# w_in rounded by GpSimd's integer add and split by ScalarE's copy and VectorE's subtraction, in place of sums on TensorE

## The chip, the core and the metric

The kernel runs on one core of one Trainium2 chip. The core's engines are TensorE (PE in the profile, its weight loads PEld), VectorE (DVE), ScalarE (ACT), GpSimd (POOL) and SyncE (SP), which here issues all DMA transfers. The metric is the device time of one execution in microseconds (us). The kernel before took 1277.62 us, the median of three runs from 1276.24 to 1278.96.

## The reference

Three blocks follow each other. The inputs have 8 batches of 8 heads with 576 rows of 64; the rows come out as 4608 tokens of 512.

```python
k_p, v_p = mean of k, v over groups of 8 rows              # 72 pooled rows
attn = softmax(q @ k_p.T / sqrt(64)) @ v_p                 # attention
x = attn as (4608, 512)
h = x @ w_in                                               # first MLP, w_in (512, 1024)
solu = h * softmax(h);  x = layernorm(solu) * g_ln @ w_out
out = ((x @ w1) * (x @ w2)) @ w3 @ w_out                   # second MLP
```

The weights of both MLPs arrive as 64-bit floats; the kernel reads them as pairs of 32-bit words and rounds them to 32-bit floats itself. Matrix products run on pairs of reduced floats (a high part and the low rest), three products for each.

## The kernel before

**Stages.** First come attention and the first MLP, interleaved by an order written out by hand; then the second MLP. The work is cut into slots. A function is put into a slot with `put`, sixteen slots make one unit of 256 tokens, and `HEAVY` names the products that TensorE does in each slot. The instructions of TensorE and the DMA issues of SyncE stand in that order. Those of VectorE, ScalarE and GpSimd are put in order by a scheduler within what the dependences allow. Each engine then works through its own row of instructions strictly in order.

**The first 50 us.** The heavy products cannot begin before two things are there: w_in, and the attention output of the first 256 tokens. The attention of these tokens has two halves of 128 tokens. For each half ScalarE takes exponentials of the scores (line 487), GpSimd multiplies them with the reciprocals of their sums (lines 507 and 514, the products called pr), TensorE transposes the products (pt, px), ScalarE copies the rounded high part (pth, line 539) and VectorE subtracts it for the low part (ptl, line 543). GpSimd also sums the tail of v (line 300) and spreads it over heads (vlh and VLL, lines 422 and 423). Then twenty products called av (line 571) follow on TensorE, and after them the first products with w_in (line 602).

**Rounding w_in.** w_in (`Win`) is cut into eight pieces of 128 by 512, numbered 0 to 7. For each piece SyncE loads 512 KB (line 157). ScalarE, for pieces 3 and 5 VectorE, takes the absolute value of the upper words; VectorE clamps it (line 206), shifts it (line 207) and merges sign and top bit into it (line 213), masks the exponent out of it (line 214) and scales the lower words with that (line 215). ScalarE copies the upper part rounded to the reduced format (`upper`, line 218). TensorE adds upper part, minus the copy, and lower part in PSUM with products against the identity and its negative (`store`, lines 223 to 225), and ScalarE copies the sum as the low rest (line 226). The slots of the loads and steps are `WIN_SLOTS`, those of `store` `WIN_STORE`.

**Rounding the other weights.** `Rounded`, which w_out, w1, w2, w3 and the last matrix use, does it otherwise: GpSimd scales the lower words to an integer (line 168), VectorE clamps, shifts and merges (lines 173, 174 and 177), and GpSimd adds the two as integers (`total`, line 183).

Of the kernel before, what the change touches and what calls it, by code (L numbers as in the profile page):

```python
# [8 lines left out]
F32 = mybir.dt.float32  # L9
F32R = mybir.dt.float32r  # L10
I32 = mybir.dt.int32
U32 = mybir.dt.uint32
AF = mybir.ActivationFunctionType
ALU = mybir.AluOpType
# [4 lines left out]
def attention_moe_kernel(  # L19
# [25 lines left out]
    nc = tc.nc  # L45

    B, H, S, D = q.shape
    P = 128
# [14 lines left out]
    F64_LO = 2.0**-15  # L63
    F64_HI = 122879.9921875

    PSUM = bass.MemoryType.PSUM
    const = ctx.enter_context(tc.tile_pool(name="const", bufs=1))
# [8 lines left out]
    def bankm(name):  # L76
        return PS.tile([P, 512], F32, tag="bm", name=name, bufs=3)
# [3 lines left out]

    ident = const.tile([P, P], F32, tag="ident", name="ident")
    make_identity(nc, ident)
    negid = const.tile([P, P], F32R, tag="negid", name="negid")
    nc.scalar.activation(negid, ident, AF.Copy, scale=-1.0)

    mask8 = const.tile([P, H], F32, tag="mask8", name="mask8")
    m16 = const.tile([P, 16], F32, tag="m16", name="m16")
# [10 lines left out]
    def split(hi, lo, src):  # L99
        nc.scalar.activation(hi, src, AF.Copy)  # L100
        nc.vector.tensor_tensor(lo, src, hi.bitcast(F32), ALU.subtract)

    def weight_pair(pool, tag, shape, name):
        return (
            pool.tile(shape, F32R, tag=tag + "h", name=name + "h"),
            pool.tile(shape, F32R, tag=tag + "l", name=name + "l"),
        )
# [6 lines left out]
    def at(t, i):  # L114

        n = t.shape[2] // 512
        return t[:, i // n, (i % n) * 512 : (i % n) * 512 + 512]
# [11 lines left out]
    def put(slot, fn, *args, first=5):  # L129
        assert now is None or slot > now  # L130
        events.setdefault(slot, []).append((first, len(events.get(slot, ())), fn, args))
# [19 lines left out]
    class Rounded:  # L151
# [13 lines left out]
        def bits(self):  # L165

            m, b, hi = self.m, self.b, self.hi = *self.scratch(), self.t[:, :, 1]
            nc.gpsimd.tensor_scalar(m, self.t[:, :, 0].bitcast(U32), 2.0**-29, 1.0, ALU.mult, ALU.mult)
            if self.abs_on_act:
                nc.scalar.activation(b.bitcast(F32), hi.bitcast(F32), AF.Abs)  # L170
            else:
                nc.vector.tensor_scalar(b, hi, 0x7FFFFFFF, None, ALU.bitwise_and)
            nc.vector.tensor_scalar(b.bitcast(F32), b.bitcast(F32), F64_LO, F64_HI, ALU.max, ALU.min)
            nc.vector.tensor_scalar(b, b, 3, 0x3FFFFFFF, ALU.logical_shift_left, ALU.bitwise_and)

        def rest(self):
            nc.vector.scalar_tensor_tensor(self.b, self.hi, -0x40000000, self.b, ALU.bitwise_and, ALU.bitwise_or)  # L177
# [8 lines left out]
    win = weight_pair(wp, "w16", [P, 4, F], "win")  # L186
    gw = [M.tile([P, FC, C], F32R, tag=t, name=t, bufs=1) for t in ("gwh", "gwl")]

    class Win(Rounded):
# [5 lines left out]
        def scratch(self):  # L195
            return [S1.tile([P, 512], I32, tag=t, name=t, bufs=4) for t in ("cvm", "cvb")]

        def bits(self):

            m, b = self.m, self.b = self.scratch()  # L200
            mf = m.bitcast(F32)
            if self.abs_on_act:
                nc.scalar.activation(mf, self.t[:, :, 1].bitcast(F32), AF.Abs)
            else:
                nc.vector.tensor_scalar(m, self.t[:, :, 1], 0x7FFFFFFF, None, ALU.bitwise_and)
            nc.vector.tensor_scalar(mf, mf, F64_LO, F64_HI, ALU.max, ALU.min)
            nc.vector.tensor_scalar(b, m, 3, 0x3FFFFFFF, ALU.logical_shift_left, ALU.bitwise_and)

        def rest(self):

            m, b, hi, lo = self.m, self.b, self.t[:, :, 1], self.t[:, :, 0]
            mf = m.bitcast(F32)
            nc.vector.scalar_tensor_tensor(b, hi, -0x40000000, b, ALU.bitwise_and, ALU.bitwise_or)
            nc.vector.tensor_scalar(m, b, -0x800000, None, ALU.bitwise_and)
            nc.vector.scalar_tensor_tensor(mf, lo.bitcast(U32), 2.0**-52, mf, ALU.mult, ALU.mult)

        def upper(self):
            nc.scalar.activation(at(win[0], self.i), self.b.bitcast(F32), AF.Copy)

        def store(self):  # L220
            hi, lo = at(win[0], self.i), at(win[1], self.i)
            s = bankm(f"w{self.i}")
            nc.tensor.matmul(s, ident, self.b.bitcast(F32), start=True, stop=False)
            nc.tensor.matmul(s, negid, hi, start=False, stop=False)
            nc.tensor.matmul(s, ident, self.m.bitcast(F32), start=False, stop=True)
            nc.scalar.activation(lo, s, AF.Copy)

    class Gw(Rounded):

# [448 lines left out]

    H0 = (-9, 2)
    T0 = (8, 13)  # L680
    WIN_STORE = (-31, -27, -25, -24, -22, -20, -18, -17)

    WIN_SLOTS = (-44, -38, -33, -31, -29, -26, -24, -21)
    GW_SLOTS = range(-8, 24, 4)
    KEPT_SLOTS = 22, 236
# [3 lines left out]

    def convert(pc, s_, load=None):  # L690
        put(s_ - 5 if load is None else load, pc.load, first=5 if load is None else 8)
        if isinstance(pc, Win):
            steps = (pc.bits, 0), (pc.rest, 1), (pc.upper, 2), (pc.store, WIN_STORE[pc.i] - s_)
        else:
            steps = (pc.bits, 0), (pc.rest, 1), (pc.total, 2), (getattr(pc, "store", None), 3)
        for fn, i in steps:
            if fn:
                put(s_ + i, fn, first=8)

# [29 lines left out]
    for i, pc in enumerate(pieces(Win, w_in) + gws):  # L729
        pc.abs_on_act = i in ABS_ON_ACT  # L730
        if i < 8:
            convert(pc, WIN_SLOTS[i], -47 + i)
        else:
            convert(pc, GW_SLOTS[i - 8])
# [6 lines left out]
    for i, pc in enumerate(bg):  # L741
        convert(pc, KEPT_SLOTS[0] + (KEPT_SLOTS[1] - KEPT_SLOTS[0]) * i // len(bg))
    units = [Unit(u) for u in range(NU)]
    for un in units:
        s_ = SLOTS * un.u
# [138 lines left out]
    for m in range(FC):  # L884
# [6 lines left out]
        if m in BLOCKS_AT:  # L891
            i = BLOCKS_AT.index(m)
# [206 lines left out]
```

## Time and profile before

| | |
|---|---|
| median of three runs | 1277.62 us (1276.24 to 1278.96) |
| the profiled execution | 1279.12 us, of which its span is 1277.3 us |
| TensorE busy | 1232.1 us (96%) |
| VectorE, ScalarE, GpSimd busy | 755.5 us (59%), 525.8 us (41%), 432.9 us (34%) |
| chain that ended last | TensorE 69%, VectorE 12%, DMA 9%, ScalarE 3%, GpSimd 2% |

The share of busy time is over the whole span. The change touches about the first 45 us, so the rows below are mostly from there: the chain of waits (followed back from the last instruction, at each step to what released it), the groups of instructions by form, and single instructions in order of time. A row in order of time gives start and duration in us; a bracket at its end gives how long the engine sat idle before it and what ended that.

### The profile page before, as it was taken

Reading aid. Unit: us, or ns where it says so; the run is one execution under the profiler, and the core shown is the slowest. Engines: PE = TensorE matmul, PEld = TensorE weight load, DVE = VectorE, ACT = ScalarE, POOL = GpSimd, SP = SyncE. Lnnn points to the kernel's source line nnn. Section 1 sums busy time; section 2 is a strip of 40 time slices with the busy share of each in tenths; the row PEclk is TensorE's granted clock in tenths of the full one; section 3 lists DMA queues with packets and bytes.
Section 4 is the critical chain, followed back from the end, with each engine's and each line's share of the span. In section 5 each row is a group of like instructions: output and inputs, shape, how many; then the busy total and the mean of one; then the engine's idle time right before and its main releaser. Section 6 shows DMA issues by size and latency. Waiting matters only on the chain.

```text
span 1277.3 us, 21834 instructions
## 1 busy us (share of the span) xinstructions
PE 1232.1 (96%) x8278; PEld 1125.1 (88%) x8278; DVE 755.5 (59%) x1497; ACT 525.8 (41%) x1480; POOL 432.9 (34%) x547
## 2 busy tenths in 40 slices
PE   7879999999999999999999999999999999999998
PEld 5668889898889888988998899999999999999997
DVE  6777576766767675545357555555454545454544
ACT  5654666665666666644344221212121212121211
POOL 3444535353535353310000142515152524242411
PEclk9989999999999999999999999999999999999999
DMA  9564546464646454214033102020101020101000
GB/s 231 123 153 116 140 130 159 117 163 116 160 133 165 131 164 107 83 42 140 26 131 117 33 1 67 1 67 1 67 1 67 2 66 1 67 1 67 5 31 34
DMA packets 85753, 109.42 MB, mean 86 GB/s; under 512 B 43664, under 2 KB 43664, under 8 KB 85648
## 3 DMA queue, kind: packets, MB, share of 16 engines
q1 hardware_dynamic: 85648, 108.03, 30.2%
q8 instruction: 65, 1.06, 0.4%
q14 instruction: 40, 0.33, 0.1%
HBM read 78.65 MB, written 29.36 MB: 85 GB/s over the span
## 4 chain that ended last, share of the span: by engine, by line
PE 69%; DVE 12%; DMA 9%; ACT 3%; issue 3%; POOL 2%; SPq 2%; POOLq 0%; DVEq 0%; ACTq 0%
PE p L959 9%; PE p L961 9%; PE p L960 9%; PE h L602 7%; PE acc L1005 5%; PE acc L1008 5%; PE acc L1007 5%; DMA f<-in_moe_w_dram 4%; PE x L660 3%; PE x L661 2%; PE x L659 2%; DMA f<-in_moe_w_out_dram 2%; DMA kv<-in_v_dram 2%; PE lt L645 2%; PE av L571 2%
## 5 line engine op out<-in xcount | busy, mean ns | idle before, releaser
L979 POOL TENSOR_TENSOR a<-a,b 128x256 f32<-128x256 f32 x72 | 52.9, 735 | 478.9 <-DVE b L978 478.9
L963 ACT ACTIVATE p<-p 128x256 f32<-128x256 f32 x72 | 27.9, 387 | 397.4 <-PE p L961 365.4
L659 PE MATMUL x<-lnh,gwh 128*128 128x256 f32 x576 | 167.2, 290 | 0.3 <-DVE lnl L649 0.3
L660 PE MATMUL x<-lnl,gwh 128*128 128x256 f32 x576 | 163.6, 284 | 2.5 <-DVE lnl L649 2.5
L661 PE MATMUL x<-lnh,gwl 128*128 128x256 f32 x576 | 163.5, 284 | 0.0
L660 PEld LDWEIGHTS x<-lnl,gwh 128*128 128x128 f32 x576 | 110.7, 192 | 3.8 <-DVE lnl L649 2.9
L1008 PE MATMUL acc<-wfl,ph 128*128 128x512 f32 x288 | 113.1, 393 | 0.0
L1007 PE MATMUL acc<-wfh,ph 128*128 128x512 f32 x288 | 112.9, 392 | 0.0
L659 PEld LDWEIGHTS x<-lnh,gwh 128*128 128x128 f32 x576 | 110.7, 192 | 1.7 <-DVE lnl L649 0.9
L661 PEld LDWEIGHTS x<-lnh,gwl 128*128 128x128 f32 x576 | 110.6, 192 | 0.0
L487 ACT ACTIVATE ea<-sc,mx 128x72 f32<-128x72 f32 x320 | 98.4, 332 | 15.3 <-DVE mx L484 15.3
L978 DVE TENSOR_TENSOR b<-b,p 128x256 f32<-128x256 f32 x72 | 30.2, 420 | 123.0 <-PE p L961 123.0
L602 PE MATMUL h<-winh,xh 128*128 128x512 f32 x288 | 98.5, 423 | 0.0
L602 PE MATMUL h<-winl,xh 128*128 128x512 f32 x288 | 90.0, 394 | 0.0
L602 PE MATMUL h<-winh,xl 128*128 128x512 f32 x288 | 89.4, 392 | 0.0
L507 POOL TENSOR_TENSOR pr<-ea,sm 128x512 f32<-128x512 f32 x40 | 42.8, 1070 | 122.7 <-DVE sm L503 71.4
L183 POOL TENSOR_TENSOR cvb<-cvb,cvm 128x512 int32<-128x512 int32 x48 | 62.7, 1306 | 59.9 <-DVE cvb L177 29.4
L959 PE MATMUL p<-th,w1h 128*128 128x256 f32 x288 | 81.6, 283 | 1.1 <-ACT p L963 1.1
L1005 PE MATMUL acc<-wfh,pl 128*128 128x512 f32 x288 | 82.4, 392 | 0.0
L960 PE MATMUL p<-th,w1h 128*128 128x256 f32 x288 | 81.5, 283 | 0.0
L961 PE MATMUL p<-th,w1l 128*128 128x256 f32 x288 | 81.5, 283 | 0.0
L649 DVE TENSOR_TENSOR lnl<-lt,lnh 128x512 fp32r<-128x512 f32 x72 | 49.1, 686 | 51.8 <-ACT lnh L648 51.4
(206 smaller groups left out, 3674.6 us busy)
## 6 DMA issues: line engine op xcount, KB each, us to landing
f<-in_moe_w_dram SPq DMA_DIRECT2D x32, 512.0 KB, 5.9
x2d<-xo SPq DMA_DIRECT2D x36, 256.0 KB, 2.0
xq<-x2d SPq DMA_DIRECT2D x36, 256.0 KB, 3.9
out_dram<-ot SPq DMA_DIRECT2D x36, 256.0 KB, 2.7
kv<-in_k_dram SPq DMA_DIRECT2D x32, 256.0 KB, 3.8
q<-in_q_dram SPq DMA_DIRECT2D x32, 256.0 KB, 7.7
kv<-in_v_dram SPq DMA_DIRECT2D x32, 256.0 KB, 3.7
f<-in_moe_w_out_dram SPq DMA_DIRECT2D x16, 512.0 KB, 5.9
```

The source lines that it names most:

```text
L183: nc.gpsimd.tensor_tensor(self.b, self.b, self.m, ALU.add)
L487: nc.scalar.activation(e[0:n, x], half[a][:, h], AF.Exp, bias=mx[0:n, x : x + 1], scale=1.0, accum_out=sm[0:n, x : x + 1],)
L602: nc.tensor.matmul(self.ph[:, a], s_[:, c], w_[:, c, a * 512 : a * 512 + 512], start=first, stop=last)
L659: nc.tensor.matmul(o, gw[0][:, f, ws], self.th[:, f], start=(f == 0), stop=False)
L660: nc.tensor.matmul(o, gw[0][:, f, ws], self.tl[:, f], start=False, stop=False)
L661: nc.tensor.matmul(o, gw[1][:, f, ws], self.th[:, f], start=False, stop=(f == FC - 1))
L959: nc.tensor.matmul(o, wh[:, c, fsl], th[:, c], start=c == 0, stop=False)
L960: nc.tensor.matmul(o, wh[:, c, fsl], tl[:, c], start=False, stop=False)
L961: nc.tensor.matmul(o, wl[:, c, fsl], th[:, c], start=False, stop=c == 1)
L1005: nc.tensor.matmul(accs[t], pl[:, ts], wh, start=False, stop=(fc == FC - 1))
L1007: nc.tensor.matmul(accs[t], ph[:, ts], wh, start=(fc == 0), stop=False)
L1008: nc.tensor.matmul(accs[t], ph[:, ts], wl, start=False, stop=False)
```

## The change

`Win` loses its own `bits`, `rest`, `upper` and most of `store`, and inherits the steps of `Rounded`: for each of the eight pieces GpSimd scales the lower words and adds them as integers (lines 168 and 183 of the kernel before). The result is split by `split` (lines 99 to 101): ScalarE copies the rounded high part, VectorE subtracts it. The table `WIN_STORE` and the constant `negid` go; the split stands three slots after the clamp, as for the other weights.

```diff
--- before.py
+++ after.py
@@ -81,8 +81,6 @@
 
     ident = const.tile([P, P], F32, tag="ident", name="ident")
     make_identity(nc, ident)
-    negid = const.tile([P, P], F32R, tag="negid", name="negid")
-    nc.scalar.activation(negid, ident, AF.Copy, scale=-1.0)
 
     mask8 = const.tile([P, H], F32, tag="mask8", name="mask8")
     m16 = const.tile([P, 16], F32, tag="m16", name="m16")
@@ -195,35 +193,8 @@
         def scratch(self):
             return [S1.tile([P, 512], I32, tag=t, name=t, bufs=4) for t in ("cvm", "cvb")]
 
-        def bits(self):
-
-            m, b = self.m, self.b = self.scratch()
-            mf = m.bitcast(F32)
-            if self.abs_on_act:
-                nc.scalar.activation(mf, self.t[:, :, 1].bitcast(F32), AF.Abs)
-            else:
-                nc.vector.tensor_scalar(m, self.t[:, :, 1], 0x7FFFFFFF, None, ALU.bitwise_and)
-            nc.vector.tensor_scalar(mf, mf, F64_LO, F64_HI, ALU.max, ALU.min)
-            nc.vector.tensor_scalar(b, m, 3, 0x3FFFFFFF, ALU.logical_shift_left, ALU.bitwise_and)
-
-        def rest(self):
-
-            m, b, hi, lo = self.m, self.b, self.t[:, :, 1], self.t[:, :, 0]
-            mf = m.bitcast(F32)
-            nc.vector.scalar_tensor_tensor(b, hi, -0x40000000, b, ALU.bitwise_and, ALU.bitwise_or)
-            nc.vector.tensor_scalar(m, b, -0x800000, None, ALU.bitwise_and)
-            nc.vector.scalar_tensor_tensor(mf, lo.bitcast(U32), 2.0**-52, mf, ALU.mult, ALU.mult)
-
-        def upper(self):
-            nc.scalar.activation(at(win[0], self.i), self.b.bitcast(F32), AF.Copy)
-
         def store(self):
-            hi, lo = at(win[0], self.i), at(win[1], self.i)
-            s = bankm(f"w{self.i}")
-            nc.tensor.matmul(s, ident, self.b.bitcast(F32), start=True, stop=False)
-            nc.tensor.matmul(s, negid, hi, start=False, stop=False)
-            nc.tensor.matmul(s, ident, self.m.bitcast(F32), start=False, stop=True)
-            nc.scalar.activation(lo, s, AF.Copy)
+            split(at(win[0], self.i), at(win[1], self.i), self.f)
 
     class Gw(Rounded):
 
@@ -678,8 +649,6 @@
 
     H0 = (-9, 2)
     T0 = (8, 13)
-    WIN_STORE = (-31, -27, -25, -24, -22, -20, -18, -17)
-
     WIN_SLOTS = (-44, -38, -33, -31, -29, -26, -24, -21)
     GW_SLOTS = range(-8, 24, 4)
     KEPT_SLOTS = 22, 236
@@ -689,11 +658,7 @@
 
     def convert(pc, s_, load=None):
         put(s_ - 5 if load is None else load, pc.load, first=5 if load is None else 8)
-        if isinstance(pc, Win):
-            steps = (pc.bits, 0), (pc.rest, 1), (pc.upper, 2), (pc.store, WIN_STORE[pc.i] - s_)
-        else:
-            steps = (pc.bits, 0), (pc.rest, 1), (pc.total, 2), (getattr(pc, "store", None), 3)
-        for fn, i in steps:
+        for fn, i in ((pc.bits, 0), (pc.rest, 1), (pc.total, 2), (getattr(pc, "store", None), 3)):
             if fn:
                 put(s_ + i, fn, first=8)
```

The order of the instructions changes with it on four engines; that of SyncE stays. Three places are shown. In them cvb and cvm are the scratch tiles of a piece, winh and winl the two parts of w_in, and pieces 5, 6 and 7 are cvb_301, cvb_329 and cvb_389 now; pieces 6 and 7 were cvb_347 and cvb_409, and the sums of 5, 6 and 7 on TensorE w_413, w_433 and w_440.

GpSimd before, from the first half's probability products to VLL:

```order
L507 TENSOR_TENSOR pr0_0_291<-ea0_0_262,sm0_0_261 128x512
L514 TENSOR_TENSOR pr0_0_291<-ea0_0_262,sm0_0_261 128x64 x2
L300 TENSOR_TENSOR vl0_181<-vl0_181 128x256
L300 TENSOR_TENSOR vl0_181<-vl0_181 128x128
L300 TENSOR_TENSOR vl0_181<-vl0_181 128x64
L422 TENSOR_TENSOR vlh0_337<-vl0_181,mask8_73 128x512
L507 TENSOR_TENSOR pr0_1_365<-ea0_1_314,sm0_1_313 128x512
L514 TENSOR_TENSOR pr0_1_365<-ea0_1_314,sm0_1_313 128x64 x2
L423 TENSOR_TENSOR VLL_113<-sl0_334,mask8_73 64x512
```

GpSimd now, from the second half's products on:

```order
L478 TENSOR_TENSOR pr0_1_348<-ea0_1_308,sm0_1_307 128x512
L271 TENSOR_TENSOR vl0_178<-vl0_178 128x256
L485 TENSOR_TENSOR pr0_1_348<-ea0_1_308,sm0_1_307 128x64 x2
L271 TENSOR_TENSOR vl0_178<-vl0_178 128x128
L271 TENSOR_TENSOR vl0_178<-vl0_178 128x64
L393 TENSOR_TENSOR vlh0_324<-vl0_178,mask8_71 128x512
L181 TENSOR_TENSOR cvb_301<-cvb_301,cvm_300 128x512
L394 TENSOR_TENSOR VLL_111<-sl0_321,mask8_71 64x512
L166 TENSOR_SCALAR cvm_328<-f64_183 128x512
L166 TENSOR_SCALAR cvm_388<-f64_185 128x512
L181 TENSOR_TENSOR cvb_329<-cvb_329,cvm_328 128x512
L181 TENSOR_TENSOR cvb_389<-cvb_389,cvm_388 128x512
```

Three integer adds and two scalings of lower words now stand in the same row as the second half's products and the v tail; pieces 6 and 7 end it.

ScalarE before, up to the last copy from the sums on TensorE:

```order
L226 ACTIVATE winl_102<-w4_387 128x512
L218 ACTIVATE winh_101<-cvb_347 128x512
L218 ACTIVATE winh_101<-cvb_409 128x512
L100 ACTIVATE VBDh_107<-vs1_0_395 64x2x64 x2
L226 ACTIVATE winl_102<-w5_413 128x512
L539 ACTIVATE pth0_351<-pt0_1_421 128x4x128
L540 ACTIVATE ptx0_353<-px0_1_426 128x128
L226 ACTIVATE winl_102<-w6_433 128x512
L226 ACTIVATE winl_102<-w7_440 128x512
```

ScalarE now, over the same part of the program:

```order
L168 ACTIVATE cvb_329<-f64_183 128x512
L98 ACTIVATE winh_99<-cvb_301 128x512
L168 ACTIVATE cvb_389<-f64_185 128x512
L98 ACTIVATE winh_99<-cvb_329 128x512
L98 ACTIVATE winh_99<-cvb_389 128x512
L98 ACTIVATE VBDh_105<-vs1_0_373 64x2x64
L510 ACTIVATE pth0_334<-pt0_1_395 128x4x128
L98 ACTIVATE VBDh_105<-vs1_0_373 64x2x64
L511 ACTIVATE ptx0_336<-px0_1_400 128x128
```

The copy pth of the second half stood between copies of pieces 5 and 6 taken from TensorE's sums; it now stands behind the rounded copies of pieces 6 and 7, which need GpSimd's last adds.

TensorE before, from the second half of the v sums to the first av product:

```order
L352 MATMUL vs_0_395<-kv_1_188,ident 128x128 x8
L223 MATMUL w_413<-cvb,ident 128x512
L224 MATMUL w_413<-winh,negid 128x512
L225 MATMUL w_413<-cvm,ident 128x512
L532 MATMUL pt_1_421<-ident,pr_1_365 128x128 x4
L535 MATMUL px_1_426<-ident,pr_1_365 128x128
L223 MATMUL w_433<-cvb,ident 128x512
L224 MATMUL w_433<-winh,negid 128x512
L225 MATMUL w_433<-cvm,ident 128x512
L223 MATMUL w_440<-cvb,ident 128x512
L224 MATMUL w_440<-winh,negid 128x512
L225 MATMUL w_440<-cvm,ident 128x512
```

TensorE now, the same part:

```order
L323 MATMUL vs_0_373<-kv_1_187,ident 128x128 x8
L503 MATMUL pt_1_395<-ident,pr_1_348 128x128 x4
L506 MATMUL px_1_400<-ident,pr_1_348 128x128
L542 MATMUL av_0_413<-pth_334,VBDh 128x256
L542 MATMUL av_0_413<-ptl_335,VBDh 128x256
```

The sums called w are gone, and av follows px at once.

## Rows read from the trace of the kernel before

**Rows 1.** us, busy by engine (PE to POOL), clock, DMA, GB/s

```profile
400.00:800.00 400.00, 391.26 (x2579) 355.58 (x2579) 229.12 (x430) 183.41 (x476) 93.44 (x118) 1.00 0.29 89
```

**Rows 2.** chain of waits, 10 to 95 us: start, duration, what

```profile
40.63 0.30 DVE VBDl L101
...
41.07 1.10 PE w L223 x2
...
44.34 0.86 PE w L225 x2
...
45.20 2.40 PE av L571 x20
...
50.02 1.37 PE h L602 x6
...
79.46 1.22 ACT ea L487 x8
...
88.38 0.69 DVE gwl L251
```

**Rows 3.** VectorE by form, 10 to 46 us: count, busy us, mean ns

```profile
L213 DVE SCALAR_TENSOR_TENSOR cvb<-f,cvb 128x512 int32<-128x512 int32 x8 | 6.3, 793 | 0.1
L215 DVE SCALAR_TENSOR_TENSOR cvm<-f,cvm 128x512 f32<-128x512 uint32 x8 | 5.5, 690 | 0.1
L206 DVE TENSOR_SCALAR cvm<-cvm 128x512 f32<-128x512 f32 x8 | 3.9, 489 | 7.5 <-ACT cvm L203 7.4
L207 DVE TENSOR_SCALAR cvb<-cvm 128x512 int32<-128x512 int32 x8 | 3.4, 422 | 0.1
L214 DVE TENSOR_SCALAR cvm<-cvb 128x512 int32<-128x512 int32 x8 | 3.4, 422 | 0.1
L484 DVE TENSOR_REDUCE mx<-sc 128x4 f32<-128x288 f32 x4 | 1.8, 453 | 0.0
```

**Rows 4.** ScalarE by form, 10 to 46 us

```profile
L218 ACT ACTIVATE winh<-cvb 128x512 fp32r<-128x512 f32 x8 | 5.1, 632 | 4.7 <-DVE cvb L213 4.7
```

**Rows 5.** GpSimd in order of time: start, us, engine, line, what

```profile
26.79 1.36 POOL L507 TENSOR_TENSOR pr<-ea,sm 128x512 f32<-128x512 f32 x1 [16.98 <-DVE sm L503]
...
34.99 1.03 POOL L423 TENSOR_TENSOR VLL<-sl,mask 64x512 fp32r<-64x512 f32 x1
...
40.63 0.65 POOL L168 TENSOR_SCALAR cvm<-f 128x512 int32<-128x512 uint32 x1 [4.60 <-DMA f<-in_moe_w_out_dram]
...
45.02 1.29 POOL L183 TENSOR_TENSOR cvb<-cvb,cvm 128x512 int32<-128x512 int32 x1 [3.75 <-DVE cvb L177]
...
53.66 1.04 POOL L507 TENSOR_TENSOR pr<-ea,sm 128x512 f32<-128x512 f32 x1 [0.43 <-DVE sm L503]
...
132.57 1.04 POOL L507 TENSOR_TENSOR pr<-ea,sm 128x512 f32<-128x512 f32 x1
133.57 0.55 POOL L514 TENSOR_TENSOR pr<-ea,sm 128x64 f32<-128x64 f32 x2
134.08 0.45 POOL L300 TENSOR_TENSOR vl<-vl 128x128 f32<-128x128 f32 x1
...
135.74 0.32 POOL L300 TENSOR_TENSOR vl<-vl 128x64 f32<-128x64 f32 x1
```

**Rows 6.** VectorE in order of time

```profile
16.39 0.18 DVE L397 COPY bdt<-pkl 64x32 f32<-64x32 f32 x1 [0.92 <-PE pkl L388]
...
53.28 0.20 DVE L503 RECIPROCAL sm<-sm 128x8 f32<-128x8 f32 x1
...
53.72 1.26 DVE L173 TENSOR_SCALAR cvb<-cvb 128x512 f32<-128x512 f32 x1 [0.23 <-ACT cvb L170]
```

**Rows 7.** TensorE in order of time, the wait before the row in brackets

```profile
80.72 0.41 PE L571 MATMUL av<-pth,VBDh 128*128 128x320 f32 x1 [2.36 <-ACT ea L487]
```

**Rows 8.** busy times, 82 to 86 us; clock third from the end

```profile
82.00:84.00 2.00, 2.00 (x11) 1.96 (x10) 1.85 (x6) 1.08 (x4) 0.34 (x1) 0.57 0.00 0
84.00:86.00 2.00, 2.00 (x12) 1.76 (x11) 2.00 (x8) 1.28 (x3) 2.00 (x3) 0.58 0.66 141
```

## The prediction

> **What bounds the kernel now.** I read the busy times by stretch first. From 400 to 800 us TensorE is busy 391 of 400 us at full clock [rows 1]: the reader is to see that, once the heavy products run, nothing but TensorE's own work counts, so a change of the start moves the end by as much as it moves the first heavy product. That one comes at 50.02 us, behind the twenty av products at 45.20 [rows 2]. The chain of waits shows what held av: VectorE's last low part of v ends at 40.93, then TensorE makes the sums of pieces 6 and 7 from 41.07 to 45.20, and av is the next in its row [rows 2]. Before that VectorE's conversion of w_in is the chain; its groups [rows 3] say what each step takes. Then I looked at what GpSimd does meanwhile, since the change gives it work: idle for 16.98 us until 26.79, busy without a gap to 36.02, and idle for 4.60 us until a load lands at 40.63 [rows 5].
>
> **What goes.** On TensorE 24 products of eight sums; the last two pieces alone are the 4.13 us between 41.07 and 45.20. On VectorE per piece a mask of 0.42 and a scaling of 0.69 [rows 3] for a subtraction from two tiles in SBUF, 0.69 like that of w_out [rows 2]: 0.42 us net, 3.4 us for eight. On ScalarE one copy of two goes. Were this all, av would come earlier, by at most 4.13 + 3.4 = 7.5 us.
>
> **What comes.** On GpSimd eight scalings of 0.65 and eight adds of 1.29 [rows 5], 15.5 us, beside the 9.23 us from 26.79 to 36.02. That fits into its idle time; the dependences are the trouble: each piece now goes VectorE merge, GpSimd add, ScalarE copy, VectorE subtraction, and each engine works strictly in its order. In the orders shown, the second half's products and the v tail share GpSimd's row with pieces 5 to 7, and ScalarE's pth copy stands behind the rounded copies of pieces 6 and 7. So av, which had to wait for VectorE and TensorE, now waits for GpSimd's very last add for w_in. I follow this path in three legs, first without any mutual disturbance. Clamp and shift are 0.42 each, a merge 0.69 (the means of lines 206 and 213 hold delayed ones), a row maximum 0.45 [rows 3], a copy on ScalarE 0.63 [rows 4], a reciprocal 0.20 [rows 6], the scaling before it as much.
>
> Leg 1, to the first half's products. VectorE's small copy for k at 16.39 [rows 6] stands ahead of the merge of piece 1, which ends at 17.3; handover 0.14 (as from 40.93 to 41.07 [rows 2]), add 1.29, copy 0.63, subtraction 0.69: 20.05. Behind it in VectorE's row up to the reciprocal stand three clamps or masks, two shifts, a maximum, a merge, the scaling and the reciprocal: 3 x 0.42 + 2 x 0.42 + 0.45 + 0.69 + 0.2 + 0.2 = 3.65, and a handover. The products start at 23.9, where they now start at 26.79 [rows 5]. So far the change gains 2.9 us.
>
> Leg 2, to the second half's products. GpSimd: products 1.04 and 0.55, scaling 0.65, add of piece 3 1.29 = 3.53. ScalarE copies it (0.63), VectorE subtracts (0.69) and only then merges piece 4 (0.69), GpSimd adds (1.29), ScalarE copies (0.63). Then VectorE has a subtraction, a mask, the scaling, a clamp and the reciprocal (0.69 + 0.42 + 0.2 + 0.42 + 0.2 = 1.93), beside which ScalarE's last three of four exponentials (three quarters of 1.22 [rows 2]) are hidden. With 0.4 for handovers that is 9.8: 33.7.
>
> Leg 3, to av, is GpSimd's row as printed: 1.04, the v tail's first sum (0.7, between the 0.45 of half its size and the 1.04 of twice), 0.55, 0.45, 0.32, vlh 1.04 (the size of pr), add of piece 5 1.29, VLL 1.03, two scalings 1.30, two adds 2.58 [rows 5] = 10.3. ScalarE then copies piece 7 (0.63), a quarter of a microsecond of v, and pth (0.6); VectorE subtracts ptl (0.69) and av's second product can run. With handovers 12.7: 46.4, so 1.2 us later than 45.20. The gain of leg 1 is used up and more.
>
> **Mutual disturbance.** The trace shows what VectorE and GpSimd do to each other. A clamp of 0.42 took 1.26 at 53.72, until just before the products that began at 53.66 ended at 54.70 [rows 5, 6]. GpSimd suffers too: the row from pr to VLL printed for before would take 6.7 us by the undisturbed durations of leg 3 (1.04 + 0.55 + 0.7 + 0.45 + 0.32 + 1.04 + 1.04 + 0.55 + 1.03) and took 9.23 [rows 5], a factor of 1.37. GpSimd's part of legs 2 and 3 is 3.53 + 1.29 + 10.3 = 15.1 us. Undisturbed it adds nothing; with that factor it adds 5.6 and av comes at 52.0. Below nothing it cannot go, as the durations are the shortest seen. VectorE's row in legs 2 and 3 is made largely of the same operations as in that stretch, but it also stands waiting for ScalarE, and then disturbs nobody. I take two thirds, 3.7 us: av at 50.1, 4.9 late.
>
> The Trainium skill, "SBUF — State Buffer", section "Who interferes with whom", says that of the two the second to issue fully blocks until the first ends. The 1.26 us row agrees. By that rule alone the whole 5.6 would stand, and av would be 6.8 late.
>
> **The clock.** With the sums gone, TensorE has little to do between the first scores and av: v sums and transpositions, with pauses. The trace shows what such a pause does: after a wait of 2.36 us [rows 7] the granted clock of 82 to 86 us is 0.57 and 0.58 [rows 8], that is (0.43 + 0.42) x 2 / 0.5 = 3.4 us at 1.2 instead of 2.4 GHz with TensorE busy, half of which, 1.7, is lost. Here the stretch would fall on av, the queries' transposition and the scores, all on the path. I cost one such stretch, 1.7 us; none is the lower end, two (3.4) the upper.
>
> "TensorE: Matmul & The Clock Gate" of the Trainium skill, section "What's actually happening", calls the slow state the default that activity lifts. By that the loss is sure. The rows above show the fall, but not at this place.
>
> **What costs nothing.** The k tail's small sums move behind the first scaling on GpSimd, and are still done before the pooling of k on TensorE that the copy at 16.39 waits for. The loads of pieces 6 and 7 now wait for a scaling and a merge of pieces 0 and 1, which end no later than the scaling on VectorE they waited for; SyncE's row is unchanged, so nothing behind them moves. The conversion of w_out's third part slips behind the scores' maxima; the part after it, still to be loaded, is later anyway.
>
> **Sum.** +1.2 (path) + 3.7 (disturbance) + 1.7 (clock) = +6.6 us. After 50 us the orders are the same but for that third part, so I see nothing that gives it back. The profiled execution took 1279.1 (span 1277.3); it would take 1285.7. Its median sister runs took 1277.6, so the forecast is 1284.2.
>
> **Rivals.**
> *GpSimd keeps up* (faster). If the last rounded copy is done by some 40 us, as VectorE's last low part was, pth no longer waits and the removed sums show: 4.1 less 1.7 for the clock, to 7.5 with the VectorE time: 1270.1 to 1275.2, about 1273. For it: GpSimd's 16.98 and 4.60 us of idle time [rows 5] hold the 15.5 us of new work. Against: three legs without disturbance already give 46.4, because the waits lie between the steps. It decides where GpSimd's last add for w_in ends: by 39.5 it wins, as ScalarE's copy then ends at about 40.
> *Little disturbance, clock held* (no change). Path and at most 1.4 us of the rest, or a microsecond or two saved in a leg: 1275.1 to 1280.2. For it: the mean shift (0.42 [rows 3]) shows that many such operations are not delayed. Against: the 1.37.
> *Everything in full*: 1.2 + 5.6 + 3.4 = 10.2, 1287.8, and 1289.5 if a pause later on lets the clock fall once more.
>
> **Chances.** What a measurement of this kernel tells from no change is about 0.2%, 2.6 us. Forecast (1280.2 to 1286.5) 0.48; everything in full, from 1286.5 on, 0.19; little disturbance 0.20; GpSimd keeps up 0.13. So slower 0.67, same 0.20, faster 0.13. The range from 1276.0 to 1289.5 leaves the faster case and a little above outside; the likeliest case's own is 1280.2 to 1286.5.
>
> **What would show it.** Right: in the chain of waits of the changed kernel, from 15 to 50 us, GpSimd's adds and ScalarE's copies stand where VectorE and TensorE stood; the first products start before 26.79, the second half's after 33; the last add for w_in ends between 44 and 48; av starts behind ptl at 46 to 52; VectorE's clamps and merges reach over 1 us there; the clock is 0.5 for some microseconds around av. From the first heavy product on, the same intervals as before. Wrong: av before 45; pth not waiting for the copies ahead of it; or a shift at av that is no longer there at 100 us, which would mean that a load or wait between had slack.

## The result and the profile after

| | kernel before | changed kernel |
|---|---|---|
| median of 4 runs | 1276.98 us (1276.24 to 1278.96) | 1286.86 us (1286.0 to 1287.65) |
| ratio, 95% interval | 1 | 1.0081 [1.0057, 1.0104] |
| profiled execution, span | 1279.1, 1277.3 | 1287.65, 1285.9 |
| mean granted clock | 0.996 | 0.985 |

The change costs 9.9 us by the medians and 8.6 by the spans; the forecast was 6.6 (1284.2). The shift arises ahead of the first heavy product: first scores +7.86 us (48.77 before, 56.63 after), and by the same products +7.5 at 62 us and +8.2 from 80 to 125. Up to 620 us it then moves between 7.7 and 10.4, as small waits fall differently in the two traces (the largest after 165 us is one of 1.98 us at 600 in the kernel before), and from 660 us to the end it is +8.2. In this pair of traces nothing is given back.

The two traces do not begin alike. ScalarE's absolute value of the first piece of w_in, with which the conversion begins, waits for that piece's load, and the load landed 0.72 us earlier in the trace of the changed kernel (first the kernel before, then the changed one):

```profile
10.04 0.66 ACT L203 ACTIVATE cvm<-f 128x512 f32<-128x512 f32 x1 [8.03 <-DMA f<-in_moe_w_in_dram]
9.32 0.67 ACT L168 ACTIVATE cvb<-f 128x512 f32<-128x512 f32 x1 [7.32 <-DMA f<-in_moe_w_in_dram]
```

Counted from this first step, the scores come at 38.73 us before and at 47.31 now, 8.6 us later in place of 7.9.

The chain of waits of the changed kernel, from the second half's products to the first h (start, duration, what), to be laid beside [rows 2]:

```profile
34.55 1.10 POOL pr L478
...
39.21 1.54 POOL cvb L181
40.75 0.02 issue
40.77 0.64 ACT winh L98
...
42.39 1.12 DVE cvb L175
43.52 0.80 DVE cvb L171
44.31 0.02 issue
44.33 1.38 DVE cvb L172
45.71 0.02 issue
45.73 0.70 DVE cvb L175
...
46.57 1.59 POOL cvb L181
48.16 0.02 issue
48.18 0.64 ACT winh L98
48.82 0.02 issue
48.84 0.69 DVE winl L99
49.53 0.03 issue
49.56 0.28 DVE VBDl L99
49.84 0.61 DVE ptl L514
50.45 0.04 issue
50.50 4.59 PE av L542 x19
55.09 0.87 PE pq L422 x4
```

Where VectorE and TensorE stood before, the add of piece 5 (L181), ScalarE's copy, VectorE's merges of pieces 6 and 7 (L175), the add of piece 7, and its copy and subtraction stand in a row. ScalarE in order of time shows why pth is in it: it is behind both copies, not held by its own transposes, which were done before 39 us.

```profile
45.45 0.63 ACT L98 ACTIVATE winh<-cvb 128x512 fp32r<-128x512 f32 x1 [3.49 <-POOL cvb L181]
48.18 0.63 ACT L98 ACTIVATE winh<-cvb 128x512 fp32r<-128x512 f32 x1 [2.10 <-POOL cvb L181]
49.01 0.58 ACT L510 ACTIVATE pth<-pt 128x512 fp32r<-128x512 f32 x1
```

GpSimd in order of time, against [rows 5]: the first products at 24.07 in place of 26.79, then adds of 1.57 and 1.58 where 1.29 is the undisturbed one.

```profile
24.07 1.37 POOL L478 TENSOR_TENSOR pr<-ea,sm 128x512 f32<-128x512 f32 x1 [0.62 <-DVE sm L474]
...
39.17 1.57 POOL L181 TENSOR_TENSOR cvb<-cvb,cvm 128x512 int32<-128x512 int32 x1
...
46.57 1.58 POOL L181 TENSOR_TENSOR cvb<-cvb,cvm 128x512 int32<-128x512 int32 x1 [1.15 <-DVE cvb L175]
```

TensorE, the wait before a row in brackets, and then the granted clock by stretch (third number from the end): 11.15 us of waiting, and the half clock from 45 to 55 us, which lies on all of av. The nineteen products last 4.59 us, where the twenty of before lasted 2.40 [rows 2].

```profile
49.64 0.58 PE L542 MATMUL av<-pth,VBDh 128*128 128x256 f32 x1 [11.15 <-ACT pth L510]
```

```profile
40.00:45.00 5.00, 0.00 (x0) 0.00 (x0) 4.55 (x5) 1.18 (x2) 4.76 (x5) 0.76 1.07 241
45.00:50.00 5.00, 0.36 (x1) 0.29 (x1) 3.12 (x6) 2.13 (x5) 2.65 (x3) 0.50 0.24 73
50.00:55.00 5.00, 4.72 (x21) 4.41 (x21) 3.52 (x8) 1.03 (x3) 0.00 (x0) 0.50 0.00 0
```

### The profile page after: what moved, and what is told of

The parts are those of the page before. It is cut to its first block, busy times and chain, and to the rows that moved or that the text cites. A ratio compares the mean times of both kernels' runs of the same rounds, so it can differ in the third digit from the quotient of the medians.

```text
span 1285.9 us, 21757 instructions
## 1 busy us (share of the span) xinstructions
PE 1224.7 (95%) x8238; PEld 1125.7 (88%) x8238; DVE 757.3 (59%) x1489; ACT 520.2 (40%) x1471; POOL 448.7 (35%) x563
## 3 DMA queue, kind: packets, MB, share of 16 engines
q8 instruction: 65, 1.06, 0.4%
## 4 chain that ended last, share of the span: by engine, by line
PE 74%; DVE 9%; DMA 7%; ACT 3%; issue 3%; POOL 2%; SPq 1%; ACTq 0%; POOLq 0%; DVEq 0%
PE p L924 9%; PE p L926 9%; PE p L925 9%; PE h L573 9%; PE acc L970 5%; PE acc L973 5%; PE acc L972 5%; DMA f<-in_moe_w_dram 5%; PE x L631 3%; PE x L632 3%; PE x L630 3%; PE av L542 2%; PE lt L616 2%; PE sc L437 1%; DVE e L588 1%
## 5 line engine op out<-in xcount | busy, mean ns | idle before, releaser
L181 POOL TENSOR_TENSOR cvb<-cvb,cvm 128x512 int32<-128x512 int32 x56 | 74.0, 1321 | 70.1 <-DVE cvb L175 39.9
```

Source lines behind the costliest of these rows:

```text
L181: nc.gpsimd.tensor_tensor(self.b, self.b, self.m, ALU.add)
```

## The experiments

Single executions differ: 29 runs of the kernel before lie between 1270.05 and 1280.54. Each ratio is to runs of the kernel before that belong to the experiment (median 1275.30 for e1 to e4, 1276.29 for e5 to e8). So beside the ratio each experiment is read at two places of its trace: av's second product, which needs ptl, and the first scores. The time between them is 3.61 us in the kernel before, at full clock.

The first step, when the first piece of w_in has landed, lies between 9.32 and 11.02 us in these traces, and this scatter is carried along: the changed kernel, e2, e3, e1 and e5 have the same order up to there and begin at 9.32, 9.93, 10.40, 10.65 and 10.68, and their second half's products on GpSimd start at 34.54, 35.17, 35.61, 35.87 and 35.89. So the table also gives the scores counted from the first step. In e1, e2, e3, e5 and e8 three later steps of the w_out pieces are held in their old places.

| kernel | first step | av's second product | first scores | scores from first step | between the two places | ratio to before, 95% interval |
|---|---|---|---|---|---|---|
| before | 10.04 | 45.16 | 48.77 | 38.73 | 3.61 | 1 |
| changed | 9.32 | 50.50 | 56.63 | 47.31 | 6.13 | 1.0081 [1.0057, 1.0104] |
| e1, nine products to fill the wait | 10.65 | 51.87 | 57.41 | 46.76 | 5.54 | 1.0092 [1.0064, 1.0120] |
| e2, copies of pieces 6, 7 behind pth | 9.93 | 48.04 | 53.95 | 44.02 | 5.91 | 1.0067 [1.0043, 1.0092] |
| e3, pieces 6, 7 behind ptl | 10.40 | 44.01 | 50.29 | 39.89 | 6.28 | 1.0036 [1.0021, 1.0051] |
| e4, before with load on GpSimd | 9.54 | 54.83 | 58.44 | 48.90 | 3.61 | 1.0106 [1.0074, 1.0137] |
| e5, thirteen products | 10.68 | 51.89 | 55.97 | 45.29 | 4.08 | 1.0094 [1.0071, 1.0117] |
| e6, GpSimd on 8 of 512 columns | 10.27 | 43.55 | 48.99 | 38.72 | 5.44 | 1.0008 [0.9995, 1.0022] |
| e7, before without the sums | 11.02 | 44.30 | 50.19 | 39.17 | 5.89 | 1.0010 [0.9996, 1.0023] |
| e8, pieces 5 to 7 behind pth | 9.68 | 40.62 | 46.89 | 37.21 | 6.27 | 1.0017 [1.0000, 1.0033] |

**e2: only the copies move.** In the changed kernel the split of pieces 6 and 7 is queued behind the second half's ptx:

```diff
-            nc.scalar.activation(x, px, AF.Copy)
+            ix = nc.scalar.activation(x, px, AF.Copy)
+            if self.a == 0 and t == 1:
+                behind.append(ix)
...
-            split(at(win[0], self.i), at(win[1], self.i), self.f)
+            with tc.issue_after(getattr(behind[0], "ins", behind[0])) if behind else ExitStack():
+                split(at(win[0], self.i), at(win[1], self.i), self.f)
```

> The changed kernel, with the split (ScalarE's copy and VectorE's subtraction) of w_in's pieces 6 and 7 queued behind the second half's pth and ptx instead of ahead of them; the integer operations and GpSimd's adds of these pieces stay where they are, the instructions are the same. Theory "rows" (av is late because pth and ptl stand behind the last two rounded copies): pth is free to go at about 42, ptl behind the last merge of piece 7 at about 46.4, so av's second product at about 47.2 in place of 50.50, and the time is 3.0 to 3.8 us shorter, 1283.1 to 1283.9. Rival "disturbance" (the same instructions on VectorE and GpSimd slow each other in any order, and this is what costs the 8 us): av moves by less than 1 us, time 1286 to 1287.5.

TensorE in order of time:

```profile
43.42 0.58 PE L549 MATMUL av<-pth,VBDh 128*128 128x256 f32 x1 [3.69 <-ACT pth L515]
48.04 0.58 PE L549 MATMUL av<-ptl,VBDh 128*128 128x256 f32 x1 [4.04 <-DVE ptl L521]
```

pth is free 6.2 us sooner, and av's second product then waits 4.04 us for VectorE, whose row still has the merges of pieces 6 and 7 ahead of ptl. Scores come 2.7 us earlier, 3.3 counted from the first step. The time was expected 3.0 to 3.8 us shorter; the ratio is 1.0067, and its interval overlaps that of the changed kernel, so the time does not show the gain. The rival, by which av moves less than 1 us, is out. ScalarE's copies are one of two rows that hold av.

**e3: the pieces' whole work moves.** Absolute value, clamp, shift, merge and split of pieces 6 and 7 are queued behind ptx and its subtraction.

```diff
+        late = {6: -17, 7: -16}.get(pc.i) if isinstance(pc, Win) else None
+        if late:
+            s_ = late
...
-                put(s_ + i, fn, first=8)
+                put(s_ + i, *((pc.late, fn) if late else (fn,)), first=8)
```

> The changed kernel, with everything that ScalarE and VectorE do for w_in's pieces 6 and 7 (absolute value, clamp, shift, merge, split) queued behind the second half's pth, ptl and ptx; same instructions. Theory "rows": ptl no longer stands behind the merges, av waits only for VLL and starts at 41 to 42.5, the two pieces are rounded beside av and scores and their last split ends at about 48.5, ahead of the last fourth of h that reads it (about 52.5), so the first h stands at 49 to 50, 8 us sooner, and the time is 1277.5 to 1280, within 0.3% of the kernel before. If half the shift was disturbance that follows the instructions, 1281 to 1283. Rival "disturbance" alone: 1285.5 to 1287.5. A loss of its own would be h waiting for the late pieces: TensorE idle ahead of the products with winl of pieces 6 and 7, up to 3 us.

Scores come 6.3 us sooner than in the changed kernel (7.4 from the first step) and the ratio falls to 1.0036, where "disturbance alone" wanted 1285.5 or more. Most of the disturbance is still there: from 5 to 60 us VectorE's 128x512 operations took 5.1 us more than undisturbed, 6.3 in the changed kernel (e4 says how this is counted), though part of it now lies beside av. So it is mostly the order of the rows that turns the changed kernel's GpSimd time into a late av. The forecast of 41 to 42.5 us for av was missed: it starts at 42.99, since piece 5's add and copy still stand ahead of pth, and the time, 1280.88, is above the expected 1277.5 to 1280. And half clock remains: 6.28 us between the two places. ScalarE in order of time:

```profile
41.53 0.63 ACT L98 ACTIVATE winh<-cvb 128x512 fp32r<-128x512 f32 x1 [2.08 <-POOL cvb L183]
42.19 0.27 ACT L98 ACTIVATE VBDh<-vs 64x128 fp32r<-64x128 f32 x1
42.36 0.58 ACT L520 ACTIVATE pth<-pt 128x512 fp32r<-128x512 f32 x1
```

**e4: the load alone.** The kernel before, with the eight scalings and adds on scratch:

```diff
+            nc.gpsimd.tensor_scalar(self.d, self.t[:, :, 0].bitcast(U32), 2.0**-29, 1.0, ALU.mult, ALU.mult)
...
+            nc.gpsimd.tensor_tensor(self.d, hi, self.d, ALU.add)
```

> The kernel before, with GpSimd's eight scalings and eight integer adds of the change run on scratch that nobody reads, so that the load on GpSimd and on its port with VectorE is there but no instruction of another engine waits for it. Rival "disturbance" (load on GpSimd slows VectorE, and GpSimd's own products come later in its row): av from 45.20 to 48 to 50, time 1280 to 1284. Theory "rows" (the load costs little by itself, the price is that the rounded copies wait for the adds and pth waits for the copies): av at 45.2 to 46.7, time 1277 to 1278.8.

Both were too low: nobody reads what these instructions write, and the only wait for one of them in the trace is 0.4 us of a load, and yet scores are 9.7 us late and the ratio is 1.0106. VectorE first, then GpSimd, in order of time:

```profile
41.81 2.77 DVE L208 TENSOR_SCALAR cvm<-cvm 128x512 f32<-128x512 f32 x1
...
45.29 1.51 DVE L209 TENSOR_SCALAR cvb<-cvm 128x512 int32<-128x512 int32 x1
```

```profile
41.22 1.57 POOL L426 TENSOR_TENSOR VLL<-sl,mask 64x512 fp32r<-64x512 f32 x1
42.76 0.29 POOL L517 TENSOR_TENSOR pr<-ea,sm 128x64 f32<-128x64 f32 x1
43.01 1.28 POOL L215 TENSOR_TENSOR dum<-f,dum 128x512 int32<-128x512 int32 x1
```

A clamp of 0.42 stood from 41.81 to 44.58, across three GpSimd instructions, and ended 0.29 us after the last of them. From 5 to 60 us VectorE's 128x512 operations with one input (0.42 undisturbed) took 9.7 us more than that in all, those with two (0.69) 2.5 more; in the kernel before it is 1.9 and 1.3, in the changed one 4.1 and 2.2. So e4 has 9.1 us more of this than the kernel before, most of the 9.7 by which scores are late, as VectorE is the chain there. Of the 9.7 us, 3.9 came ahead of the first half's products, at 30.70 in place of 26.79 [rows 5] although GpSimd had been idle for 6.70 us: their reciprocal on VectorE was late. GpSimd's own row shows at one place: the sums of the v tail, behind two scratch instructions, keep ScalarE waiting for 2.43 us and VectorE behind it for 1.03.

The Trainium skill, "SBUF — State Buffer", section "Who interferes with whom", has two engines that share a port pair, of which the one that comes second blocks fully. This trace agrees for the clamps and shifts, and goes further: the clamp above stayed held past the end of the GpSimd instruction that it met, across two more. The operations with two inputs took 1.29 us at most from 5 to 60 us here, and 1.53 in any of these runs in that stretch, so they were held less.

**e6: no GpSimd time.** In the changed kernel w_in's scaling and add run on 8 of 512 columns (the low words of the others are left out), with every handover kept:

```diff
...
+            c = slice(0, 8 if isinstance(self, Win) else 512)
-            nc.gpsimd.tensor_tensor(self.b, self.b, self.m, ALU.add)
+            nc.gpsimd.tensor_tensor(self.b[:, c], self.b[:, c], self.m[:, c], ALU.add)
```

> The changed kernel, with GpSimd's scaling and add for w_in on 8 of the 512 columns only (what is left out: the low words of the other columns). Every handover VectorE to GpSimd to ScalarE stays, GpSimd's time and its load on the port go. Theory "GpSimd's time and the mutual slowing" (the 8 us are the adds' 1.26 to 1.58 us each in the row, and VectorE's instructions that are held while they run): VectorE's 128x512 instructions at 0.42 and 0.69 us nearly throughout, av at 41 to 43, scores at 48 to 49.7 with the half clock, time 1276 to 1279. Rival "handovers and order" (a chain over three engines with the copies ahead of pth is slow however short the adds are): av at 46 or later, time 1281 or more.

As the first theory said: scores at 48.99 (38.72 from the first step, 38.73 in the kernel before), ratio 1.0008. ScalarE's rows show that the handovers and the order are still there and cost little when the adds are short:

```profile
38.89 0.63 ACT L98 ACTIVATE winh<-cvb 128x512 fp32r<-128x512 f32 x1 [1.75 <-POOL cvb L183]
41.23 0.63 ACT L98 ACTIVATE winh<-cvb 128x512 fp32r<-128x512 f32 x1 [1.70 <-POOL cvb L183]
42.05 0.58 ACT L512 ACTIVATE pth<-pt 128x512 fp32r<-128x512 f32 x1
```

VectorE's excess falls from 6.3 to 1.4 us. With e4: GpSimd's time costs twice, as a link of the chain and by what it holds up on VectorE. How the 7.6 us (8.6 from the first step) between e6 and the changed kernel at the scores divide between these two was not measured apart.

**e7: the sums alone.** The kernel before without the 24 products (left out: the exact lower part):

```diff
...
-            nc.tensor.matmul(s, ident, self.b.bitcast(F32), start=True, stop=False)
-            nc.tensor.matmul(s, negid, hi, start=False, stop=False)
-            nc.tensor.matmul(s, ident, self.m.bitcast(F32), start=False, stop=True)
-            nc.scalar.activation(lo, s, AF.Copy)
+            nc.scalar.activation(at(win[1], self.i), self.m.bitcast(F32), AF.Copy)
```

> The kernel before, without the 24 products on TensorE that form w_in's lower parts (left out: the exact lower part; ScalarE copies the scaled low word in its place). GpSimd does nothing new. It tests what the removed sums are worth by themselves. Theory "sums stand in TensorE's waiting time": av no longer stands behind the last sums (45.20 in the kernel before) and starts at 42 to 43.5, but TensorE then waits there, its clock falls and av takes 4.6 us in place of 2.4: scores at 48 to 49.7 against 48.77, time within 1.5 us of the kernel before. Rival "the removed sums show" (24 products and 8 waits off TensorE's row): 1270 to 1274.

av's second product comes 0.86 us earlier, the scores 1.42 us later, half a microsecond behind what was expected. About 1 us of this is the late load: counted from the first step, av's second product comes 1.8 us earlier and the scores 0.4 later. TensorE, and its clock from 45 to 50 us in this run and then in the kernel before:

```profile
43.58 0.58 PE L566 MATMUL av<-pth,VBDh 128*128 128x256 f32 x1 [4.26 <-ACT pth L534]
```

```profile
45.00:50.00 5.00, 4.50 (x22) 4.26 (x21) 2.89 (x6) 1.65 (x3) 1.20 (x1) 0.58 0.48 103
```

```profile
45.00:50.00 5.00, 4.25 (x34) 3.97 (x33) 2.15 (x5) 2.29 (x4) 3.68 (x6) 1.00 0.46 113
```

So what the change takes off TensorE was worth nothing: the sums stood where TensorE would have waited, and with them the clock was at 2.4 GHz for av.

**e1 and e5: the clock by itself.** Nine (e1), then thirteen (e5) products that nobody reads, ahead of av in the changed kernel.

```diff
+            if self.a == 0 and t == 1:
+                wm = bankm("warm")
+                for j in range(13):
+                    nc.tensor.matmul(wm, ident, pr[:, 0:512], start=True, stop=True)
```

> The changed kernel, with nine products of the identity with the second half's softmax products (128x512 each, nobody reads the sum) queued on TensorE between the last transpose of that half and the first av product, so that TensorE has work in the 11.15 us in which it waits there. They are the only extra work; three later steps of the w_out pieces are held in their old places. Theory "rows plus clock" (av waits for ScalarE's and VectorE's in-order rows, and the long wait costs a further 2.5 us by the half clock after it): av still starts at 49.6 to 50.0 us, the 20 av products take 2.4 to 3.0 us in place of 4.6, the first h product stands at 55.0 to 55.8 in place of 57.62, and the time is 2 to 2.8 us under the changed kernel's 1286.9. Rival "clock without price" (the half clock is a by-product, the 8 us are all waiting): av and h as in the changed kernel or later by what the nine products overrun, time 1286.5 to 1288.

> As e1_clock_fill, with thirteen products in place of nine: there, the nine ended at 47.69 us, TensorE waited 3.32 us for pth, and its clock fell in the middle of av all the same, so the price of the clock was not tested. Thirteen last 11.4 us by that run's 0.44 us for half of one, up to about 50 or 51. Theory "clock has a price of its own of about 2.5 us": no half clock from 45 to 60 us; from av's second product (the first with ptl) to the first scores 3.6 to 3.9 us, as in the kernel before, in place of 6.13; time 1.5 to 2.5 us under the changed kernel's, ratio to the kernel before 1.006 to 1.007. Rival "clock without price": 5.5 us or more between these two places, ratio 1.008 or more. If the thirteen overrun pth, av starts late by the overrun and the two effects cancel; then only the distance av to scores tells.

With nine, TensorE still waited 3.32 us ahead of av. Its clock was 1.00 up to 50 us, and fell within av all the same: its products took 0.28 us until 52.92 and 0.42 from 53.20 on. That tested nothing. With thirteen:

```profile
38.84 11.33 PE L523 MATMUL warm<-pr,ident 128*128 128x512 f32 x26
51.03 0.38 PE L549 MATMUL av<-pth,VBDh 128*128 128x256 f32 x1 [0.85 <-ACT pth L513]
```

```profile
50.00:55.00 5.00, 3.54 (x25) 2.98 (x24) 4.26 (x10) 2.27 (x7) 2.47 (x5) 1.00 0.00 0
```

The clock holds, and the two places are 4.08 us apart in place of 6.13: the half clock costs 2.05 us there. Counted from the first step, the scores come 2.0 us sooner than in the changed kernel. The time says nothing of it (1.0094, where 1.006 to 1.007 was expected): both runs begin 1.3 us later than the changed kernel's trace, and the scores at about 70 us wait 3.08 us in e1 and 3.07 in e5 for ScalarE, 0.76 in the changed kernel. Whether the fill or the steps held in place make this wait was not tested. That the fill makes the kernel faster was expected and is not shown.

**e8: a version that could beat both.** e3, with piece 5's add behind VLL and its split behind ptx, and the last two splits behind the next group's qT. The split of av's first half is queued behind piece 7's merge.

```diff
...
+        d = -17 - s_ - 2 if isinstance(pc, Win) and pc.i == 5 else 0
...
+                put(-11 if late and i == 3 else s_ + i, *((pc.late, fn) if late or (d and i > 1) else (fn,)), first=8)
```

> e3_pieces_late, and also piece 5: its add on GpSimd queued behind VLL, its split behind ptx, and the last splits of pieces 6 and 7 behind the first qT of the next group; same instructions as the changed kernel. A version that could beat both. Theory "rows": pth free at 39.4 right behind sh, ptl at 40.4, VLL at 41.4, so av from 40 on in place of 42.99 and scores at 46.5 to 48 even at half clock (48.77 in the kernel before); time 1274.5 to 1276.5, ratio 0.998 to 1.001. If the late pieces hold h's last fourth, or the later maxima hold the next group's products: 1277 to 1280. Rival "disturbance alone": no better than e3's ratio of 1.0036.

```profile
39.57 0.39 PE L566 MATMUL av<-pth,VBDh 128*128 128x256 f32 x1 [0.62 <-ACT pth L527]
...
46.89 1.22 PE L452 MATMUL sc<-bdt,qT 128*128 128x144 f32 x8 [1.43 <-DVE xl L99]
```

av starts 5 us earlier than before, the scores 1.9 (1.5 from the first step), and from 80 to 125 us the difference is 0.05 to 0.7: half clock on av, 1.43 us for VectorE, where the split of av's first half now stands behind piece 7's merge, and 1.31 for a qT at 53.99 took most of it. 0.998 to 1.001 was expected; 1.0017 is at best equal. With the changed instructions no version here beats the kernel before; e6 and e7, which leave work out, don't either.

## Why the prediction was right, and where its sizes were off

Direction, range and mechanism were right; the time came 2.7 us above the forecast.

- *Leg 1.* The first products at 24.07, forecast 23.9. This is partly luck: the load of the first piece landed 0.72 us earlier than in the trace that the forecast was worked out from, and counted from there leg 1 is 0.9 longer than forecast. The forecast put no disturbance into this leg, but VectorE's scaling of the sums, taken as 0.2, took 1.23 beside an add of GpSimd from 22.14 to 23.45:

```profile
22.25 1.23 DVE L473 TENSOR_SCALAR sm<-sm 128x8 f32<-128x8 f32 x1
```

- *Leg 2.* The second half's at 34.54, forecast 33.7 without disturbance.
- *Leg 3 and disturbance.* av's second product at 50.50, forecast 50.1. The sum was right, its route not quite: I followed GpSimd's row from vlh over five adds and scalings; the chain leaves it at piece 5's add, goes over ScalarE to VectorE's merges of pieces 6 and 7, and returns for the last add, which waited 1.15 us for its merge. e2 shows the difference: with only the copies moved, VectorE's merges hold ptl.
- *Disturbance, 3.7 us.* On the chain above the two adds, a subtraction, a merge, a clamp and a shift are 2.7 us over 1.26, 0.69 and 0.42, and leg 2 is 0.7 longer than forecast: 3.4 in all, if the latter is all disturbance. I took the factor from GpSimd's side; it is VectorE that paid most (a shift of 0.42 took 1.37). One row is misread in the prediction: the clamp at 53.72 [rows 6] ended at 54.98, 0.28 us after the products that began at 53.66 had ended, not just before.
- *The clock, 1.7 us: the mis-sized term.* I took one stretch as it follows a wait of 2.36 us [rows 7, 8]. The wait here was 11.15 us, TensorE entered av at half clock, and the granted clock was 0.50 until 56 us, some 6 us of work: from av's second product to the scores 6.13 for 3.61 us, 2.5 more. e5 gives 2.05 of it back with the clock held.
- *Nothing given back.* Right in this pair of traces: +7.86 at the scores, +8.2 at the end.
- The sum from the trace is then 5.3 + 2.5 = 7.9 at the scores in place of 6.6, and 8.6 when the early load is taken out. The rest up to the medians' 9.9 (7.3 to 13.3 by the interval) is no step that these traces show, and stays open.
- *"GpSimd keeps up"* was priced wrongly: 1273 rested on the removed sums showing. e7 removes them and gains nothing, as the clock falls where they were; e6, in which GpSimd does keep up, has 1.0008. The faster case deserved a smaller chance than 0.13.

## What to carry to other kernels

Work that stands in an engine's own waiting time cost nothing here, and on TensorE it was worth its clock (e7): before taking such work away, ask what the engine will do in its place. Moving element-wise work to GpSimd beside a VectorE that is the chain cost its own time and what it held up on VectorE; read this from VectorE's longest durations, not from GpSimd's idle share. When a chain over three in-order engines makes something late, what stands ahead of the late instruction in each row is the first thing to reorder: that gave back 7.4 of 8.6 us at the scores here, counted from the first step. Before two traces are compared by the microsecond, see whether their first load landed at the same time: it differed by up to 1.7 us here.

## What the runs showed of the hardware that was not expected

GpSimd instructions whose results nobody reads made the kernel 1.06% slower (e4), and a VectorE clamp of 0.42 us took 2.77. TensorE's clock fell in the midst of av, some 2 us after it had begun again, behind a wait of 3.32 us that followed 7.89 us of continuous products at full clock (e1); behind 0.85 us it held (e5).
